# Another order for the first 48 steps of a fused attention and two-FFN kernel, with one weight stage split in two

## The chip, the cores and the metric

The kernel runs on one core of a Trainium2 chip. The metric is the device time of one execution in microseconds (us), the median of three runs. TensorE is called PE, VectorE DVE, ScalarE ACT, GpSimd POOL and SyncE SP, as in the profile.

## The reference

```python
scores = scale * q_c @ k_c.T                 # chunks of 64 tokens, 8 batches x 8 heads x 576 tokens
attn = softmax(scores);  x = attn @ v_c      # then laid out as 4608 tokens x 512
h = x @ w_in                                 # 512 -> 2048
P = a[0] + a[1]*h + a[2]*h**2 + a[3]*h**3
Q = 1.0 + abs(b[0])*abs(h) + abs(b[1])*h**2
x = (P / (Q + 1e-6)) @ w_out                 # 2048 -> 512
h = x @ w_in2;  g = s * relu(h)**2 + b2
out = g @ w_out2                             # 4608 x 512, float32
```

Weights, activations and outputs are float32. Each factor of a large product is split in a high and a low part, and a product is three matmuls: high x high, high x low, low x high.

## The kernel before

Tokens lie in 9 blocks of 512, each of four attention tiles of 128 tokens. A **step** is one block with one of 16 slices of 128 hidden columns. In the first FFN, step n has `mm1` (12 matmuls of 128x512 into one of three PSUM banks, L530 to L532), an element-wise chain that makes the rational function out of that bank, and `mm2` (12 matmuls into four accumulator banks, L548). The first 48 steps are blocks 0 and 1 with slices 0 to 7, block 2 with all 16, and the second halves of blocks 1 and 0.

No scheduler sets the order there. The table `START` is a list of tokens that `play` runs from the left; each token makes the instructions of one stage, each engine's queue gets its own in the order of the list, and semaphores hold an instruction until its inputs are there and its buffer is free. The tokens that matter, with their number:

- loads (512 KB each, v loads 256 KB in four issues): `P` q and k rows of an attention tile, `Q` the same in 16 small issues (L269), `L` and `o` its v rows (L282), `w` a weight slice. They are issued by SP, or by ACT with an `A` behind. A weight slice lies in one of four staging buffers, `wst`, until its sum is done.
- weight slice: `f` takes its absolute value on ACT (`w_abs`, L445) and scales its low words (`w_low`, L449); `g` on DVE for a pair of slices: clamp (L456), shift (L460), and top bits for each (L463); `c` the sum on POOL (L466); `d` the high part on ACT (L473); `D` or `G` the low part on DVE or POOL (L477).
- attention tile: `T`, `q`, `k` transposes and their copies (`X`, two transposes on DVE at L327, for later tiles); `S` scores; `s` maxima (L349) and subtraction (L356) by halves; `e` exponential; `m` sums; `n` normalisation on POOL, with `D` on DVE (L377); `A`, `a` transposed weights (PE, L383); `V` product with v; `v` its copy on ACT; `u` its low part on DVE (L424).
- step n: `M` mm1; `B`, `t` the absolute value and the numerator's start on ACT; `r` the denominator in two instructions on POOL (L634, L637), or with `p` and `rh` the first on ACT, or with `D` both on DVE; `l`, `E` logarithm and exponential on ACT, which divide; `b`, `N` five DVE instructions on the numerator and the quotient, of which `Nc` (L683, output `t`) is the last that reads the step's PSUM bank; `H` the high part gh on ACT; `y` the low part gl on POOL or, with `D`, on DVE (L697); `R` mm2.

With three banks, mm1 of step n+3 waits for `Nc` of step n. mm1 of steps 0 to 7 needs the four tiles 0 to 3, and so `u0` to `u3`.

The stage that the change splits reads:

```python
def w_ends(st, w):
    w_abs(st, w)
    w_low(st)
```

After step 47 come a loop body (`LOOP`) for the steps to 127, a second table (`TURN`) and a planner for the second FFN.

Of the kernel before, what the change touches and what calls it, by code (L numbers as in the profile page):

```python
# [33 lines left out]
    "w0 w1A f0 P4 w2 f1 P1 g1Pa g1Pb g1Pc c0 d0 T4a L1A T1x q1 k1 g1Pd D0 f2 S1y s1b c1 d1 w3 q4 s1d s1a k4 w4 w5 "  # L34
    "f3 P3 S4b s1c e1 s4b g3Pa g3Pb s4d T3d G1 g3Pc g3Pd m1a c2 m1b m1c P2 f4 c3 n1D f5 w6A d2 g5Pa P5 q3 s4a g5Pb "
    "P0 d3 s4c w7 g5Pc x0 e4 m4a g5Pd A1a k3 T2b c4 c5 a1 V1a S3x q2 s3b k2 d5 s3a d4 G3 s3c S2b s3d e3 w8 v1 D4 "
    "s2b L4 u1 T5d s2a G2 k5 G5 q5 L3A T0x q0 w9 s2c k0 S5a m4b S0x m4c s2d s5a n4 s5b f6 m3a P6 m3b A4d a4 s5c w10 "
    "s0a m3c s0b s5d f7 V4d s0d L0 g7Pa n3 f8 g7Pb g7Pd s0c e2 e5 A3b m5a P7A e0 f9 a3 g7Pc v4 T6b m0a q6 m5b g9Pa "
    "m5c V3c k6 c6 g9Pb n5D m2a w11 g9Pc m0b u4 m0c w12 n0D w13 Q8 c8 A5b S6a s6b L5 L2A c7 L6 T7b w14 d6 a5 w15 "
    "m2b d7 v3 m2c k7 q7 g9Pd s6a c9 s6d s6c e6 D7 m6a A0d u3 a0 d8 w16 Q9 d9 n2 S7b m6b G6 A2a a2 V2a s7a m6c f10 "  # L40
    "v2 u2 V0c v0 L7 G8 f11 u0 M0 w17 f12 g11Pa o8 M1 o9 g11Pb w18 f13 g11Pc G9 g11Pd t0 n6 c11 w19 g13Pa B0 c10 p0 "
    "r0h Q10 A6c d11 M2 s7b w20 b0a g13Pb t1 B1 p1 W0 b0b X8 b1a l0 V5a r1h E0 g13Pc s7c c12 s7d b1b e7 t2 S8b M3 "
    "N0a d10 l1 d12 s8a G11 a6 G12 m7a v5 B2 N0b f14 m7b E1 D10 N0c m7c b2a u5 n7 A7x b2b g13Pd r2 H0 s8b V6a M4 "
    "N1a s8d y0 f15 N1b v6 s8c l2 N1c t3 u6 H1 c13 g15Pa E2 b3a Q11 R0 B3 d13 N2a e8 a7 y1 g15Pb N2b D13 M5 N2c r3 "
    "B4 X9 p4 r4h t4 b3b R1 l3 M6 g15Pc g15Pd c14 H2 l4 y2 E3 f16 b4a N3a f17 b4b E4 N3b V7y c15 B5 p5 r5h m8a d14 "
    "G14 N3c g17Pa H3 t5 d15 B6 l5 y3 v7 R2 N4a N4b m8b t6 N4c g17Pb o10 b5a m8c b5b E5 n8 u7 g17Pd A8c c17 p6 r6h "
    "N5a a8 H4 N5b w21A M7 f18 l6 Q12 B7 f19 d17 S9y o11 D15 N5c g17Pc y4D c16 H5 s9a b6a s9c g19Pa b6b G17 s9b E6 "
    "R3 d16 p7 r7h g19Pb t7 y5D M8 g19Pc R4 t8 N6a b7a N6b s9d B8 X10 G16 l7 b8a N6c f20 f21 r8 o12 R5 g19Pd M9 c19 "
    "e9 b7b H6 E7 b8b g21Pa N7a t9 y6 B9 c18 m9a l8 N7b p9 r9h E8 N7c w22A H7 d19 g21Pb R6 m9b g21Pc M10 b9a d18 "
    "N8a l9 b9b c20 N8b m9c B10 y7D g21Pd E9 t10 N8c p10 N9a R7 M11 b10a c21 j7 i7 H8 N9b B11 b10b S10b N9c V8a n9 "  # L50
    "O7 r10h y8 w23A d21 s10a s10b X11 l10 s10c A9y v8 M12 s10d a9 e10 u8 V9b G18 S11a E10 t11 m10a N10a H9 G19 r11 "
    "w24 m10b v9 w25 w26 m10c B12 N10b n10 N10c s11a o13 l11 s11b s11d s11c Q13 u9 b11a f22 e11 d20 m11a f23 t12 "
    "m11b b11b E11 A10y H10 g23Pa M13 b12a r12 g23Pb m11c a10 t13 N11a N11b B13 R8 y9 l12 R9 N11c g23Pd V10y y10 "
    "n11 R10 g23Pc v10 M14 H11 A11x c23 b12b b13a p13 r13h E12 u10 b13b l13 N12a M15 E13 N12b t14 N12c y11 B14 D20 "
    "R11 H12 c22 d22 N13a a11 N13b N13c y12 V11y R12 b14a d23 t15 b14b w27A r14 H13 b15a l14 B15 D23 E14 N14a G22 "
    "v11 G21 u11 N14b M16 M17 r15 N14c b15b f24 f25 g25Pa l15 g25Pb y13D E15 g25Pd B16 r16 N15a f26 g25Pc R13 t16 "
    "f27 N15b M18 N15c g27Pa B17 H14 y14 b16a b16b H15 p17 r17h l16 t17 b17a E16 b17b N16a N16b l17 y15D c25 c24 "
    "t18 E17 R14 d24 B18 N16c g27Pb r18 g27Pd b18a N17a R15 d25 j15 N17b c27 N17c i15 g27Pc b18b H16 l18 H17 M19 "
    "c26 B19 E18 M20 w28A X12 N18a y17D y16 N18b D24 N18c t19 b19a w29A H18 B20 t20 r19 R16 l19 b19b R17 b20a r20 "
    "b20b E19 M21 y18 D25 N19a N19b l20 f28 E20 N20a N19c t21 B21 H19 R18 d27 f29 r21 b21a l21 d26 M22 b21b N20b "  # L60
    "N20c M23 O15 g29Pa E21 H20 B22 y19D w30A t22 D26 y20D N21a t23 R19 N21b N21c r22D b22a D27 b22b w31 B23 l22 "
    "b23a g29Pb E22 H21 Q14 r23 M24 N22a f30 y21 N22b N22c B24 l23 R20 b23b t24 r24 R21 E23 b24a M25 N23a N23b b24b "
    "H22 l24 E24 M26 N23c N24a y22 f31 g31Pa B25 g29Pd t25 R22 H23 b25a N24b r25 N24c H24 B26 l25 b25b g29Pc y23 "
    "E25 M27 y24 p26 r26h N25a R23 N25b t26 b26a t27 B27 b26b M28 N25c g31Pb l26 b27a E26 N26a r27 R24 H25 c28 M29 "
    "l27 y25D b27b N26b N26c E27 M30 t28 d28 b28a B28 b28b N27a R25 N27b N27c g31Pd H26 r28 B29 c29 l28 y26D t29 "
    "p29 r29h E28 D28 H27 B30 b29a c31 d29 l29 N28a b29b N28b N28c r30 g31Pc y27 G29 H28 E29 N29a c30 R26 M31 R27 "
    "t30 l30 B31 p31 r31h y28D N29b b30a d30 t31 M32 Y0 b30b E30 N29c N30a l31 d31 N30b N30c b31a b31b H29 t32 E31 "
    "N31a y29 B32 G30 H30 y30 Q15 b32a R28 b32b M33 p32 r32h B33 l32 N31b t33 R29 N31c E32 r33D l33 N32a H31 N32b "
    "M34 R30 b33a N32c y31 t34 B34 H32 M35 b33b b34a E33 b34b N33a t35 S12y N33b N33c r34D G31 l34 X13 s12b s12a "
# [12 lines left out]
)
# [1530 lines left out]
```

## Time and profile before

| | |
|---|---|
| median of 3 runs | 1639.31 us (1637.15 to 1641.09) |
| profiled execution | 1639.77 us, span 1638.0 us |
| PE busy | 1586.5 us, 97% |
| DVE busy | 1338.1 us, 82% |
| ACT busy | 1128.0 us, 69% |
| POOL busy | 608.8 us, 37% |
| moved by DMA | 263.93 MB, mean 161 GB/s |

The span runs from the first to the last instruction of the profiled execution. An engine's busy time is a sum over the whole program; where it could be faster must be read stretch by stretch. A row of the timeline gives in brackets how long the engine had been idle before the instruction, and what released it. The mean of a group of instructions is from start to end of one; two in a row can overlap by some hundredths of a microsecond.

### The profile page before, as it was taken

Reading aid. Unit: us, or ns where it says so; the run is one execution under the profiler, and the core shown is the slowest. Engines: PE = TensorE matmul, PEld = TensorE weight load, DVE = VectorE, ACT = ScalarE, POOL = GpSimd, SP = SyncE. Lnnn points to the kernel's source line nnn. Section 1 sums busy time; section 2 is a strip of 40 time slices with the busy share of each in tenths; the row PEclk is TensorE's granted clock in tenths of the full one; section 3 lists DMA queues with packets and bytes.
Section 4 is the critical chain, followed back from the end, with each engine's and each line's share of the span. In section 5 each row is a group of like instructions: output and inputs, shape, how many; then the busy total and the mean of one; then the engine's idle time right before and its main releaser. Section 6 shows DMA issues by size and latency. Waiting matters only on the chain.

```text
span 1638.0 us, 26407 instructions
## 1 busy us (share of the span) xinstructions
PE 1586.5 (97%) x9068; PEld 1293.9 (79%) x9068; DVE 1338.1 (82%) x2165; ACT 1128.0 (69%) x1909; POOL 608.8 (37%) x513
## 2 busy tenths in 40 slices
PE   4699999999999999999999999999999999999998
PEld 3577887777878888888888788888888888888886
DVE  6899988899888988888779987668867886788676
ACT  5788766667677686867678776657665756676554
POOL 3677565347577676757557510000000000000000
PEclk9799999999999999999999999999999999999999
DMA  9655302344263553625034587865589649666853
GB/s 232 158 158 147 93 1 65 84 113 134 66 167 87 154 141 83 196 65 133 3 123 135 206 272 238 324 231 174 164 208 303 233 130 297 213 220 161 279 169 86
DMA packets 365526, 263.93 MB, mean 161 GB/s; under 512 B 276816, under 2 KB 315728, under 8 KB 364880
## 3 DMA queue, kind: packets, MB, share of 16 engines
q1 hardware_dynamic: 352720, 255.55, 53.0%
q10 hardware_dynamic: 12672, 6.69, 1.5%
q8 instruction: 72, 1.18, 0.3%
q14 instruction: 62, 0.51, 0.1%
HBM read 201.33 MB, written 60.82 MB: 160 GB/s over the span
## 4 chain that ended last, share of the span: by engine, by line
PE 79%; DVE 6%; DMA 4%; ACT 4%; issue 3%; POOL 2%; SPq 2%; ACTq 0%; DVEq 0%; POOLq 0%
PE acc L548 20%; PE ae L1107 16%; PE hA L1046 11%; PE h L530 7%; PE h L532 6%; PE h L531 6%; PE hE L1046 5%; PE hc L1046 3%; PE hc L1107 3%; DMA wst<-in_moe_w_in_dram 1%; SPq L269 1%; DMA vs<-in_v_dram 1%; PE pat L383 1%; DVE ah L679 1%; PE pat L408 1%
## 5 line engine op out<-in xcount | busy, mean ns | idle before, releaser
L1107 PE MATMUL ae<-gs,wo 128*128 128x512 f32 x1152 | 294.0, 391 | 1.7 <-DVE acc L1126 0.7
L548 PE MATMUL acc<-gh,w 128*128 128x512 f32 x1152 | 288.0, 392 | 0.0
L530 PE MATMUL h<-xh,w 128*128 128x512 f32 x640 | 256.1, 400 | 8.9 <-DVE t L683 8.0
L1107 PEld LDWEIGHTS ae<-gs,wo 128*128 128x128 f32 x1152 | 215.8, 188 | 49.5 <-DVE acc L1126 1.1
L531 PE MATMUL h<-xl,w 128*128 128x512 f32 x640 | 251.0, 392 | 0.0
L532 PE MATMUL h<-xh,w 128*128 128x512 f32 x640 | 251.0, 392 | 0.0
L548 PEld LDWEIGHTS acc<-gh,w 128*128 128x128 f32 x1152 | 214.1, 188 | 44.4 <-ACT gh L691 0.2
L637 POOL TENSOR_TENSOR r<-r,ah 128x512 f32<-128x512 f32 x130 | 174.3, 1341 | 77.6 <-ACT r L632 65.0
L1046 PE MATMUL hA<-xs,wi 128*128 128x512 f32 x768 | 195.6, 390 | 0.7 <-ACT g L1057 0.7
L697 POOL TENSOR_TENSOR gl<-t,gh 128x512 fp32r<-128x512 f32 x111 | 147.7, 1333 | 100.0 <-ACT gh L691 58.4
L1046 PEld LDWEIGHTS hA<-xs,wi 128*128 128x128 f32 x768 | 144.1, 188 | 31.8 <-ACT g L1057 1.1
L1085 DVE TENSOR_TENSOR gs<-g,gs 128x512 fp32r<-128x512 f32 x224 | 146.4, 684 | 15.1 <-ACT gs L1081 14.5
L548 PE MATMUL acc<-gl,w 128*128 128x512 f32 x576 | 154.8, 390 | 2.0 <-POOL gl L697 1.9
L1081 ACT ACTIVATE gs<-g 128x512 fp32r<-128x512 f32 x224 | 132.7, 624 | 28.2 <-DVE g L1077 27.8
L530 PEld LDWEIGHTS h<-xh,w 128*128 128x128 f32 x640 | 121.2, 189 | 39.1 <-DVE t L683 12.4
L532 PEld LDWEIGHTS h<-xh,w 128*128 128x128 f32 x640 | 121.0, 189 | 26.0
L531 PEld LDWEIGHTS h<-xl,w 128*128 128x128 f32 x640 | 121.2, 189 | 24.2 <-DVE xl L424 0.3
L623 ACT ACTIVATE t<-h,a_sb 128x512 f32<-128x512 f32 x144 | 111.1, 773 | 38.1 <-PE h L532 18.1
L548 PEld LDWEIGHTS acc<-gl,w 128*128 128x128 f32 x576 | 107.6, 188 | 26.5 <-POOL gl L697 4.2
L679 DVE SCALAR_TENSOR_TENSOR ah<-r,h 128x512 f32<-128x512 f32 x144 | 98.1, 681 | 37.1 <-ACT h L668 35.7
L1128 DVE TENSOR_TENSOR acc<-ae,acc 128x512 f32<-128x512 f32 x112 | 77.0, 689 | 61.3 <-PE ae L1107 60.3
L663 ACT ACTIVATE ah<-r,lnb 128x512 f32<-128x512 f32 x144 | 103.6, 719 | 32.8 <-POOL r L637 26.5
(143 smaller groups left out, 2964.9 us busy)
## 6 DMA issues: line engine op xcount, KB each, us to landing
wi<-wq SPq DMA_DIRECT2D x112, 512.0 KB, 4.3
wo<-wq SPq DMA_DIRECT2D x112, 512.0 KB, 4.8
wst<-in_moe_w_in_dram SPq DMA_DIRECT2D x28, 512.0 KB, 5.3
wst<-in_moe_w_out_dram SPq DMA_DIRECT2D x27, 512.0 KB, 4.7
wi<-wp SPq DMA_DIRECT2D x16, 512.0 KB, 4.0
wq<-wc SPq DMA_DIRECT2D x32, 256.0 KB, 2.8
w<-wi SPq DMA_DIRECT2D x16, 512.0 KB, 6.6
raw<-x2d SPq DMA_DIRECT2D x16, 512.0 KB, 7.4
```

The costliest lines, as they stand in the source:

```text
L530: T.matmul(h, wh, xh[:, kk], start=kk == 0, stop=False)
L531: T.matmul(h, wh, xl[:, kk], start=False, stop=False)
L532: T.matmul(h, wl, xh[:, kk], start=False, stop=kk == KD - 1)
L548: T.matmul(o, l, r, start=first and n == 0, stop=last and n == 2)
L623: A.activation(t1, h_t[i], AF.Identity, scale=a_sb[:, 3:4], bias=a_sb[:, 2:3])
L637: eng.tensor_tensor(out=r, in0=r, in1=ah, op=ALU.mult)
L679: V.scalar_tensor_tensor(out=t, in0=r, scalar=ONE, in1=y, op0=ALU.add, op1=ALU.mult)
L697: (eng or (G if i < N1 else V)).tensor_tensor(out=gl, in0=tmp.pop(i)["g"], in1=f(g_t[i][0]), op=ALU.subtract)
L1046: T.matmul(ps[b], w[:, l, z * P:(z + 1) * P], x[:, z], start=n == 0 and p in (1, 2, 5), stop=n == 5, skip_group_check=True)
L1081: A.activation(gx[t, s, k][0][:, 0], gt[t, s, c], AF.Copy)
L1085: V.tensor_tensor(out=g[:, 1], in0=gt[t, s, c], in1=f(g[:, 0]), op=ALU.subtract)
L1107: T.matmul(o, w[:, e, l, dp * P:(dp + 1) * P], gx[t, 2 * u + e, k][0][:, g], start=n == 0 and p in (1, 2, 5), stop=n == 5, skip_group_chec ...
```

## The change

The table `START` is replaced by another list, said to be found for varied durations with full transfer queues counted. It makes the same stages for the same tiles, slices and steps, with two kinds of difference besides the order. Some stages change engine: `n` on DVE goes from 6 to 1, `y` on DVE from 15 to 8, `r` on DVE from 4 to 1, first instruction of `r` on ACT from 19 to 16, `D` from 13 to 11, all to POOL; weight loads that ACT issues go from 9 to 14. And `w_low` of the first FFN's slices is no longer in `f`: it is a token of its own, `h` with a letter behind.

```diff
 START = (
-    "w0 w1A f0 P4 w2 f1 P1 g1Pa g1Pb g1Pc c0 d0 T4a L1A T1x q1 k1 g1Pd D0 f2 S1y s1b c1 d1 w3 q4 s1d s1a k4 w4 w5 "
+    "w0A w1 w2 f0 f1 h1b h0b g1Pa g1Pb g1Pc g1Pd c0 c1 P2 d0 d1 P4 T2c q2 P1 G0 T4a f2 k2 w3 q4 S2d s2b P3 w4A x0 "
...
-    def w_ends(st, w):
-        w_abs(st, w)
-        w_low(st)
...
-            w_ends(st, w)
+            w_abs(st, w)
+            if phase:
+                w_low(st)
             words[n] = phase, kind, i, st, w
...
-        do["h"] = lambda n, _: w_get(n)
+        do["h"] = lambda n, x: w_low(words[n][3]) if x else w_get(n)
```

What the lists make of it stands here at three places, first before, then now. Lines of the changed kernel are up to three lower or one higher. SP's queue where it issues the v rows of tile 0 (`wst` is a weight slice, `qk` the q or k rows of a tile, `vq` v rows); before, where row 29 is those v rows:

```order
27 L253 DMA qk<-in_k_dram 128x8x64
28 L436 DMA wst<-in_moe_w_in_dram 128x4x256
29 L282 DMA vq<-in_v_dram 64x4x64 x4
30 L441 DMA wst<-in_moe_w_out_dram 128x1024
31 L436 DMA wst<-in_moe_w_in_dram 128x4x256
32 L441 DMA wst<-in_moe_w_out_dram 128x1024
33 L269 DMA qk<-in_q_dram 32x8x32 x8
34 L269 DMA qk<-in_k_dram 32x8x32 x8
35 L282 DMA vq<-in_v_dram 64x4x64 x8
```

and the part of SP's queue in the changed kernel that ends with them, in row 30:

```order
22 L442 DMA wst<-in_moe_w_out_dram 128x1024
23 L270 DMA qk<-in_q_dram 32x8x32 x8
24 L270 DMA qk<-in_k_dram 32x8x32 x8
25 L283 DMA vq<-in_v_dram 64x4x64 x4
26 L254 DMA qk<-in_q_dram 128x8x64
27 L254 DMA qk<-in_k_dram 128x8x64
28 L283 DMA vq<-in_v_dram 64x4x64 x4
29 L437 DMA wst<-in_moe_w_in_dram 128x4x256
30 L283 DMA vq<-in_v_dram 64x4x64 x4
```

Before, the 16 small issues of tile 8 stand behind the v rows of tile 0; now they stand ahead of them, with two other sets of v rows, a tile's q and k rows and a weight slice between.

DVE around `u0` (the last `xl<-pat,xh`), where the rows after it lead to step 0's `b` (`t<-t,h`); before:

```order
78 L424 TENSOR_TENSOR xl<-pat,xh 128x4x64 x2
79 L424 TENSOR_TENSOR xl<-h,xh 128x4x64
80 L424 TENSOR_TENSOR xl<-pat,xh 128x4x64
81 L456 TENSOR_SCALAR w<-w 128x1024
82 L460 TENSOR_SCALAR w<-w 128x1024
83 L463 SCALAR_TENSOR_TENSOR w<-wst,w 128x512 x2
84 L456 TENSOR_SCALAR w<-w 128x1024
85 L349 TENSOR_REDUCE mx<-pat 128x4
86 L657 TENSOR_TENSOR t_878<-t_878,h 128x512
```

and now:

```order
62 L425 TENSOR_TENSOR xl<-h,xh 128x4x64
63 L425 TENSOR_TENSOR xl<-pat,xh 128x4x64
64 L474 TENSOR_TENSOR w_3_749<-w,w_3_749 128x512
65 L453 TENSOR_SCALAR w<-w 128x1024
66 L457 TENSOR_SCALAR w<-w 128x1024
67 L350 TENSOR_REDUCE mx<-pat 128x4
68 L460 SCALAR_TENSOR_TENSOR w<-wst,w 128x512 x2
69 L453 TENSOR_SCALAR w<-w 128x1024
70 L654 TENSOR_TENSOR t_873<-t_873,h 128x512
```

`u0` stands some 17 rows nearer to the start of DVE's queue, and about as many weight and attention instructions as before lie between it and step 0.

POOL where step 0's denominator is made (`e<-e,sm` is a normalisation, `w<-w,wst` a weight sum, `r` a denominator); before:

```order
20 L477 TENSOR_TENSOR w_3_743<-w,w_3_743 128x512
21 L377 TENSOR_TENSOR e<-e,sm 128x512
22 L466 TENSOR_TENSOR w<-w,wst 128x512 x2
23 L637 TENSOR_TENSOR r<-r,ah 128x512 x2
24 L466 TENSOR_TENSOR w<-w,wst 128x512
25 L477 TENSOR_TENSOR w_4_914<-w,w_4_914 128x512
26 L477 TENSOR_TENSOR w_7_1010<-w,w_7_1010 128x512
```

and now:

```order
27 L378 TENSOR_TENSOR e<-e,sm 128x512
28 L631 TENSOR_SCALAR r<-ah,ab_sb 128x512
29 L634 TENSOR_TENSOR r<-r,ah 128x512
30 L463 TENSOR_TENSOR w<-w,wst 128x512 x2
31 L474 TENSOR_TENSOR w_6_909<-w,w_6_909 128x512
32 L474 TENSOR_TENSOR w_4_984<-w,w_4_984 128x512
33 L463 TENSOR_TENSOR w<-w,wst 128x512 x2
34 L634 TENSOR_TENSOR r<-r,ah 128x512 x2
```

Step 0's denominator is now wholly on POOL, and six weight instructions stand between it and those of steps 1 and 2, where before steps 0 and 1 stood together.

## Rows read from the trace of the kernel before

**Rows 1.** The page: PE's busy time, and its busy tenths in 40 slices.
```profile
PE 1586.5 (97%) x9068; PEld 1293.9 (79%) x9068; DVE 1338.1 (82%) x2165; ACT 1128.0 (69%) x1909; POOL 608.8 (37%) x513
...
PE   4699999999999999999999999999999999999998
```

**Rows 2.** Stretches: us, busy PE, PEld, DVE, ACT, POOL, clock, DMA share, GB/s.
```profile
0.00:60.84 60.84, 31.47 (x505) 24.16 (x505) 42.42 (x87) 37.81 (x73) 27.75 (x27) 0.86 0.87 216
60.84:139.25 78.41, 70.59 (x561) 56.50 (x561) 74.80 (x133) 67.09 (x119) 59.36 (x47) 0.93 0.55 140
139.25:179.65 40.40, 40.40 (x240) 32.98 (x239) 36.28 (x61) 33.36 (x59) 27.21 (x23) 1.00 0.38 109
179.65:353.01 173.36, 172.01 (x1013) 138.40 (x1012) 146.82 (x237) 116.85 (x192) 93.81 (x77) 1.00 0.29 75
```

**Rows 3.** Timeline of PE: start, us, instruction, in brackets the idle time before.
```profile
60.84 0.79 PE L530 MATMUL h<-xh,w 128*128 128x512 f32 x1 [0.80 <-ACT xh L416]
...
77.43 0.79 PE L530 MATMUL h<-xh,w 128*128 128x512 f32 x1 [3.41 <-DVE t L683]
...
96.79 0.50 PE L530 MATMUL h<-xh,w 128*128 128x512 f32 x1 [0.49 <-DVE t L683]
...
138.84 0.66 PE L383 MATMUL pat<-ident,e 128*128 128x128 f32 x4 [1.40 <-POOL e L377]
...
293.54 0.27 PE L339 MATMUL h<-qkT 64*64 64x64 f32 x2 [0.49 <-DVE t L683]
...
359.54 0.50 PE L530 MATMUL h<-xh,w 128*128 128x512 f32 x1 [0.93 <-DVE t L683]
```

**Rows 4.** Waits of DVE up to 61 us: total, times, longest.
```profile
DVE w L456 <- ACT w L445: 6.9, 1, 6.9
DVE mx L349 <- PE pat L339: 4.5, 2, 3.6
```

**Rows 5.** Groups by line to 350 us: busy us, mean ns, idle before.
```profile
L637 POOL TENSOR_TENSOR r<-r,ah 128x512 f32<-128x512 f32 x44 | 59.7, 1356 | 27.3 <-ACT r L632 23.1 <-DVE t L657 2.1
...
L466 POOL TENSOR_TENSOR w<-w,wst 128x512 int32<-128x512 int32 x32 | 44.6, 1400 | 33.8 <-DVE w L463 17.9 <-ACT w L445 3.8 <-DVE sm L371 3.5
L697 POOL TENSOR_TENSOR gl<-t,gh 128x512 fp32r<-128x512 f32 x32 | 43.3, 1354 | 37.7 <-ACT gh L691 18.9 <-PE acc L548 11.7 <-DVE e L356 5.2
...
L463 DVE SCALAR_TENSOR_TENSOR w<-wst,w 128x512 int32<-128x512 int32 x32 | 25.7, 815 | 0.1
...
L634 POOL TENSOR_SCALAR r<-ah,ab_sb 128x512 f32<-128x512 f32 x25 | 21.4, 855 | 30.5 <-ACT ah L617 30.3
...
L477 DVE TENSOR_TENSOR w<-w,w 128x512 fp32r<-128x512 f32 x13 | 12.7, 976 | 2.0 <-ACT w L473 2.0
L377 POOL TENSOR_TENSOR e<-e,sm 128x512 f32<-128x512 f32 x11 | 12.0, 1087 | 5.4 <-DVE sm L373 4.7 <-ACT gh L691 0.7
...
L327 DVE STREAM_TRANSPOSE qkT<-qk 128x512 f32<-128x512 f32 x18 | 11.7, 684 | 0.0
L456 DVE TENSOR_SCALAR w<-w 128x1024 f32<-128x1024 f32 x16 | 11.2, 697 | 7.0 <-ACT w L445 6.9
L697 DVE TENSOR_TENSOR gl<-t,gh 128x512 fp32r<-128x512 f32 x14 | 11.0, 787 | 0.0
...
L349 DVE TENSOR_REDUCE mx<-pat 128x4 f32<-128x256 f32 x25 | 10.0, 413 | 5.7 <-PE pat L339 4.7 <-PE h L339 1.0
...
L377 DVE TENSOR_TENSOR e<-e,sm 128x512 f32<-128x512 f32 x5 | 5.3, 1051 | 0.1
```

**Rows 6.** SP: its longest wait up to 61 us, and issues of `Q8`.
```profile
SPq L436 <- POOL w L466: 8.6, 2, 7.4
...
55.61 3.55 SPq L269 DMA_DIRECT2D qk<-in_q_dram  x7
...
61.15 3.90 SPq L269 DMA_DIRECT2D qk<-in_k_dram  x8
```

**Rows 7.** Timeline: POOL and DVE at the subtraction of L477.
```profile
31.79 4.19 POOL L477 TENSOR_TENSOR w<-w,w 128x512 fp32r<-128x512 f32 x3
...
33.12 1.73 DVE L477 TENSOR_TENSOR w<-w,w 128x512 fp32r<-128x512 f32 x1 [0.16 <-ACT w L473]
```

95 rows, old and new, of the table START are left out of this document.

## Prediction

> **What bounds the kernel now.** I read the slices of the page first [rows 1]: TensorE (PE) is at 9 tenths or more from the third slice to the last but one, so over 37 of 40 slices only its own work counts, and it can be shortened only where it waits. Its busy time is 1586.5 of 1638.0 us. The 51.5 us left are almost all in the part that the change rewrites. The table by stretch [rows 2] says where: up to 60.84 us, where the first matmul of step 0 starts (I call the start of the first matmul of step n "Mn"), PE is busy 31.47 us; from M0 to M13 it is busy 70.59 of 78.41; from M13 to M19 it is never idle; from M19 to M48 it lacks 1.35 of 173.36.
>
> Who holds it up is in the timeline [rows 3]: M3 and M6 each start after a wait for `DVE t L683`, the last vector instruction of a step three earlier, which gives that step's PSUM bank back. So look next at DVE in the same table [rows 2]: 74.80 of 78.41 busy from M0 to M13. In that stretch DVE is the bound and PE follows it. From M13 on DVE has air (36.28 of 40.40, then 146.82 of 173.36) and PE is the bound. Before M0 neither is: DVE is busy 42.42 of 60.84, its longest waits being 6.9 us for the first weight and 4.5 for PE [rows 4], and behind those stand the transfers, at 87% of their engines and 216 GB/s [rows 2]. So three questions make the sum: when M0 starts, how much DVE work lies between M0 and M13, and which small waits are left after that. After step 48 the order is untouched.
>
> The profiled execution took 1639.77 us, a span of 1638.0 and 1.77 around it; the median is 1639.31, 0.46 lower. I make the sum against 1639.77 and take 0.46 off at the end. About 0.2%, 3.3 us, can be told from no change.
>
> **1. The start of step 0.** M0 needs all four attention tiles of token block 0; the last vector instruction for it is `u0` (L424), and DVE works in order, so M0 comes after all DVE work listed before `u0`. Counted over the two lists up to `u0`, the change takes away three normalisations (n on DVE, L377, 1.05 us each, [rows 5]: 3.15) and five of the half-tile softmax instructions (0.41 each: 2.07), adds one tile's two transposes at L327 (2 x 0.68: 1.37), and has one softmax sum less, three small instructions that I put at 0.6: together 4.5 us less. With the same 18.4 us idle, M0 would be at 60.84 - 4.5 = 56.3. The other gate is the last transfer that M0 needs. In the new list this is `L0`, the v rows of tile 0; ahead of it and with it stand w0 to w10, P0 to P7 and Q8 (20 loads of 512 KB) and five v loads of 256 KB, 11,520 KB or 11.8 MB; at 216 GB/s they are through at 54.6, and the second product of tile 0, the copy on ACT and `u0` follow in some 2.3 us: 56.9. I take **56.6, 4.2 earlier**. Bounds: the last v loads stand on SP behind sixteen issues of Q8, which took 0.5 us of SP each [rows 6], behind L4, and behind w10, which waits for its buffer; SP's longest waits so far are for exactly that (8.6 us on `POOL w L466`, [rows 6]). If these give the whole gain back, M0 stays at 60.8. On the other side, DVE has 11.5 us of idle time besides the first 6.9; a third less and M0 is at 52.5.
>
> The split of the weight's first stage (`w_low` now placed by itself as `h`) is in this term. The 32 instructions of L449 stay on ACT, but the clamp on DVE no longer stands behind two of them. What hides them now is that the POOL sum (L466) needs them only after three DVE instructions. If ACT is late with one, POOL waits, and the buffer and the next load with it. ACT also issues 14 weight loads in place of 9; ACT does nothing else while one waits for its buffer. I cost both at nothing beyond the bounds above.
>
> **2. From M0 to M13.** M13 needs the bank of step 10. Between `u0` and `N10c`, the last DVE instruction of step 10, the two lists have the same 33 instructions of steps (three for each of 0 to 10), the same b, u and D. The change has five softmax halves more here (2.07), one weight pair more (clamp 0.70, shift about the same, and twice 0.82: some 3.05), one normalisation more (1.05), one tile's transposes less (1.37) and one gl less on DVE (0.79), [rows 5]: **4.0 us more**. It is work that was not done before M0. Against it stand 3.6 us in which DVE is idle in this stretch now [rows 2], most of it waiting just after M0 for steps 0 to 2; the new list puts more than ten weight and softmax instructions between `u0` and `N0c`, which can fill these waits, so I let 2.1 of it go and keep 1.5. Both ends, all of it kept and none, are in the range. The stretch then takes 78.4 + 4.0 - 2.1 = 80.3, and M13 is at 136.9 in place of 139.25: of the 4.2 us only **2.35** are left.
>
> **3. From M13 to M19** PE is the bound in both [rows 2]: six mm1 and eight mm2 in both lists, and one transposition of the attention weights more (0.6 to 0.66, [rows 3]): 2.35 - 0.6 = 1.75 left.
>
> **4. After M19.** Over the whole list DVE gives up seven gl (0.79 each) and five normalisations (1.05), and some smaller things: 10.8 us by these two alone. From step 16 to 46 each step's last DVE instruction then stands behind less DVE work than now, where from M19 to M48 26.5 of 173.4 us are idle already. So the four short waits for DVE, the longest of them 0.49 us [rows 3], 1.2 together, should go, and so should the 0.93 at M50: **2.1 us**. What is late next is POOL, which takes these over: five normalisations at 1.09, seven gl at 1.35, and six more first halves (0.86) and three more second halves (1.36) of the denominator, [rows 5], 24 us on an engine that is busy 93.8 of 173.4 us there [rows 2]. It has room on average, and I cost this at nothing.
>
> Sum: 1.75 + 2.1 = 3.9 us less; 1639.77 - 3.9 - 0.46 = **1635.4**.
>
> **Rivals.**
> *POOL becomes the bound between M0 and M13 (slower).* POOL is busy 59.36 of 78.41 us there now. The new list adds there two weight sums and two low parts of weights (L466, L477, some 1.4 us each), a gl (1.35) and two whole denominators (2.21) in place of three second halves (1.36), and takes a normalisation out (1.09): 6.2 us more, 84%. A step's chain runs ACT, POOL, ACT, DVE, so a late POOL makes every third bank late. And DVE itself lengthens beside a busy POOL: at 33.12 us DVE took 1.73 us for the subtraction at L477, POOL being in L477 from 31.79 on; the mean on DVE is 976 ns, against 787 for the same form at L697 [rows 5, 7]. If all 6.2 us come to lie on the path, M13 is at 143.1, the rest of POOL's load keeps the 2.1 us of waits alive, and with 0.65 for the transposition the kernel ends 4.5 later, at 1643.8. With the 2.1 us kept alive the result is 1.8 us less plus what is exposed: the gain is gone from 1.8 us exposed, and the kernel is slower by over 0.2% from 5.1. The Trainium skill, "SBUF — State Buffer", section "Who interferes with whom", has a rule for this: a DVE instruction with two SBUF inputs and a GpSimd one that reads SBUF exclude each other for a whole instruction. The row at 33.12 us agrees with it (1.73 us). By that rule the moved subtractions no longer exclude POOL from DVE's side, while those that stay meet a POOL that is busier; no run here shows what of the 6.2 us would meet one, so it changes neither the price nor the chance. Chance of this rival 0.14.
>
> *All of the early start is eaten (no change).* DVE is saturated from M0 to M13, and the work not done before M0 is 4.0 us; if the 3.6 us idle stay, M13 is at 56.6 + 78.4 + 4.0 = 139.0, as now. Then 0.25 - 0.65 + 2.1 = 1.7 us are won: 1637.6. Chance 0.28.
>
> *The idle time shrinks too (much faster).* M0 at 52.5 and no DVE idle to M13: 4.1 + 1.5 more, 1629.8. For it speaks that eleven of the 18.4 idle us are waits between engines in a list where three pairs of stages stand close together. Against it: transfers at 87%. Chance 0.18.
>
> That the list leaves out or repeats work is ruled out by counting: step for step the two hold the same operations, apart from the engine of some and the split stage.
>
> **Chances and range.** Forecast, 3 to 6 us faster or a little less, 0.40. Faster by over 0.2%: 0.18, and 0.34 of the forecast's (its own spread goes below 3.3 at times): 0.52. Slower: 0.12 of the POOL rival's 0.14, and 0.02 for a late SP load: 0.14. Within 0.2%: 0.34. Range 1629.0 (the faster rival, and a little of the loop's waits) to 1642.0 (most of the way to the POOL rival).
>
> **What would show it.** In the trace after: M0 near 56.6, with `L0`'s landing just before; DVE busy about 38 us up to it; M3 near 72 and M6 near 95, still waiting for DVE; M13 near 137; no DVE wait of PE from M19 to M50. Wrong, if M0 is at 60 or later (SP), if M3 to M13 wait for an instruction whose releaser is POOL, or if gl on POOL holds mm2 (L548) up.

## The result: slower, and the profile after

The changed kernel takes 1649.92 us (median of 4, 1648.35 to 1652.21), the kernel before 1640.2 beside it: a ratio of 1.0064, 95% interval 1.005 to 1.0078. The profiled execution took 1648.81 us with a span of 1647.0, 9.0 us more than before.

I cut both traces at M0, M19, M48 and M51. At M19, M48 and M51 the two orders have done the same matmuls; at M0 nearly so (the old list has one tile's four transpositions more, and the scores of another tile). Single steps between don't compare. Nor does M22, which I first took for a common point: the old list has the 12 matmuls of step 18's `mm2` ahead of it, the new one behind. The expectations below still speak of M22; I use it only among versions of one list. After M51 the difference hardly changes. The table by stretch, first the two stretches of the kernel before that [rows 2] does not have, then the changed kernel (columns: stretch, its length, then for PE, PEld, DVE, ACT and POOL busy us and count; the granted clock, where 1.00 is the 2.4 GHz level; DMA share; GB/s):

```profile
60.84:179.65 118.81, 110.99 (x797) 89.48 (x798) 111.08 (x192) 100.45 (x177) 86.58 (x69) 0.95 0.49 130
353.01:369.66 16.65, 15.72 (x130) 12.55 (x128) 16.12 (x26) 9.93 (x17) 6.58 (x6) 1.00 0.50 114
```

```profile
0.00:63.11 63.11, 32.60 (x501) 25.89 (x501) 35.35 (x80) 36.38 (x70) 29.62 (x28) 0.82 0.93 213
63.11:188.64 125.53, 112.40 (x802) 89.17 (x801) 116.07 (x198) 101.03 (x178) 99.17 (x77) 0.97 0.51 129
188.64:359.13 170.49, 170.29 (x1013) 138.55 (x1011) 136.43 (x216) 115.17 (x189) 102.86 (x89) 1.00 0.26 68
359.13:379.22 20.09, 17.11 (x135) 13.58 (x129) 17.70 (x28) 11.68 (x18) 7.75 (x7) 0.92 0.49 103
```

Read the lengths first: +2.3 to M0, +6.7 from M0 to M19, -2.9 from there to M48, +3.4 from M48 to M51, together 9.6 (0.6 of it comes back later). From M19 to M48 the new list gains: for the same 1013 matmuls PE idles 0.20 us in place of 1.35. DVE has 10.4 us less to do there and POOL 9 more, and PE is the bound. Then read DVE (third engine) up to M19: it is busy 151.4 us in place of 153.5, so the list does take work off it; but it idles 37.2 (188.64 less 151.42) in place of 26.2 (179.65 less 153.50). That is the loss.

How well does a stretch repeat? Three profiles of the changed order (this one and two of experiment 6, whose edits come after 330 us) have M0 at 62.56 to 63.52 and M19 at 188.64 to 190.85; three of the old order have them at 60.13 to 60.95 and 178.82 to 179.65. So up to M19 differences of 1 or 2 us say little. From M19 to M48 an order repeats to 0.1 us.

The waits of DVE up to M0 (answering to [rows 4]; columns: total us, times, longest), one of the kernel before, then the changed one:

```profile
DVE xl L424 <- ACT xh L416: 1.6, 1, 1.6
```

```profile
DVE xl L425 <- ACT xh L417: 7.7, 4, 3.2
DVE w L453 <- ACT w L446: 6.8, 1, 6.8
DVE mx L350 <- PE h L340: 5.8, 1, 5.8
DVE sm L369 <- ACT e L363: 3.9, 2, 3.5
```

The second is the first weight, as before. The first has grown by 6.1 us: `u` waits for `v`, which waits for the product with the v rows, and those come late. The issues of `L0` before; then SP's queue in the changed kernel and the last wait of PE ahead of M0 (columns: start, us, what; x8 is eight issues in a row):

```profile
46.89 2.58 SPq L282 DMA_DIRECT2D vq<-in_v_dram  x4
```

```profile
33.11 7.96 SPq L270 DMA_DIRECT2D qk<-in_q_dram  x8
41.12 5.30 SPq L270 DMA_DIRECT2D qk<-in_k_dram  x8
46.46 2.58 SPq L283 DMA_DIRECT2D vq<-in_v_dram  x4
50.36 3.05 SPq L283 DMA_DIRECT2D vq<-in_v_dram  x4
54.10 2.58 SPq L283 DMA_DIRECT2D vq<-in_v_dram  x4
60.10 0.33 PE L409 MATMUL pat<-eT,vq 64*64 64x64 f32 x2 [1.15 <-DMA vq<-in_v_dram]
```

Q8's sixteen issues hold SP from 33.1 to 46.4, 13.3 us, and the three sets of v rows that M0 needs (L1, L4, L0) go out behind them; the last, `L0`, at 54.1 to 56.7, 7.2 us later than before. I had written them through at 54.6.

### The profile page after: what moved, and what is told of

The parts are those of the page before. It is cut to its first block, busy times and chain, and to the rows that moved or that the text cites. A ratio compares the mean times of both kernels' runs of the same rounds, so it can differ in the third digit from the quotient of the medians.

```text
span 1647.0 us, 26450 instructions
## 1 busy us (share of the span) xinstructions
PE 1587.4 (96%) x9068; PEld 1296.6 (79%) x9068; DVE 1326.9 (81%) x2145; ACT 1126.5 (68%) x1906; POOL 633.4 (38%) x536
## 4 chain that ended last, share of the span: by engine, by line
PE 78%; DVE 5%; DMA 5%; POOL 3%; ACT 3%; SPq 3%; issue 3%; DVEq 0%; POOLq 0%; ACTq 0%
PE acc L545 19%; PE ae L1104 16%; PE hA L1043 11%; PE h L527 7%; PE h L529 6%; PE h L528 6%; PE hE L1043 5%; PE hc L1043 3%; PE hc L1104 2%; DMA wst<-in_moe_w_in_dram 2%; DMA qk<-in_q_dram 1%; SPq L270 1%; POOL r L634 1%; PE pat L409 1%; SPq L283 1%
## 5 line engine op out<-in xcount | busy, mean ns | idle before, releaser
L694 POOL TENSOR_TENSOR gl<-t,gh 128x512 fp32r<-128x512 f32 x118 | 157.0, 1333 | 82.7 <-ACT gh L688 55.0
L1125 DVE TENSOR_TENSOR acc<-ae,acc 128x512 f32<-128x512 f32 x112 | 77.1, 690 | 60.8 <-PE ae L1104 59.8
L620 ACT ACTIVATE t<-h,a_sb 128x512 f32<-128x512 f32 x144 | 111.2, 772 | 18.9 <-PE h L529 12.1
```

Of the source, the lines that this page charges most:

```text
L620: A.activation(t1, h_t[i], AF.Identity, scale=a_sb[:, 3:4], bias=a_sb[:, 2:3])
L694: (eng or (G if i < N1 else V)).tensor_tensor(out=gl, in0=tmp.pop(i)["g"], in1=f(g_t[i][0]), op=ALU.subtract)
```

## The experiments

Each edit moves tokens of `START` or changes their engine letters; a line of the diffs is the piece of the list. Times are medians; before, measured beside them, lies between 1638.9 and 1639.9.

**1. Where Q8 stands.** First the token alone.

```diff
-... m4b c4 Q8 d4 m3c ... w10 g7Pb L0 w11 ...
+... m4b c4 d4 m3c ... w10 g7Pb L0 Q8 w11 ...
```

> The changed kernel with one token moved: Q8 (16 small loads) stands behind L0, the v rows of tile 0, and no longer five loads ahead of them. Theory (the queue ahead of L0): in the changed kernel SP issues Q8 from 33.1 to 46.4 us and the pieces of L0 only from 54.1 to 56.7; without these 13.3 us the pieces go out some 10 us earlier, M0 comes at 56 to 58 in place of 63.1, and since VectorE's work up to step 10 stays what it is, M13 moves by the same 5 to 6 us: 1644 to 1645 us. Rival (POOL is the bound from M0 to M13): M0 comes earlier, but M13 stays near 146 and the time at 1648 to 1650. Second rival (the transfers themselves are the limit, not their order in the queue): M0 stays at 61 to 63 and the time at 1648 to 1650.

1655.52 us, ratio 1.0093 (1.0076 to 1.011): slower still, M0 at 66.68. All three expectations missed. DVE's timeline shows why:

```profile
57.95 0.71 DVE L328 STREAM_TRANSPOSE qkT<-qk 128x512 f32<-128x512 f32 x1 [9.33 <-DMA qk<-in_k_dram]
61.47 0.71 DVE L328 STREAM_TRANSPOSE qkT<-qk 128x512 f32<-128x512 f32 x1 [2.81 <-DMA qk<-in_k_dram]
```

These are X8, the transposes of those rows. The new list has X8 ahead of `u0`, so a later Q8 holds DVE itself. Q8 must be moved with its consumers.

```diff
-... Q8 d4 ... X8 V1b ... f13 S8b s6b ... b0b M1 ... S7a b1a ...
+... d4 ... L0 Q8 w11 ... b0b X8 M1 ... S7a S8b b1a ...
```

> The changed kernel with all of tile 8's early part behind the first token block: Q8 stands behind L0, its two VectorE transposes X8 behind b0b (after M0, about where the old list has them), its scores S8 behind S7a. The run with Q8 alone moved had VectorE wait 9.3 and 2.8 us for these loads at X8, ahead of u0, which hid what the queue does. Theory (SP's queue ahead of L0 holds M0): M0 at 57 to 59 in place of 63.1, M13 at 140 to 142 in place of 146.2, the time 1644 to 1646 us. Rival (the transfers as a whole limit the start, whatever their order): M0 at 61 to 63, 1648 to 1650.

1651.59 us, ratio 1.0074 (1.0056 to 1.0092). M0 comes at 56.74, just ahead of the theory's 57 to 59, but M3 at 84.46 and M22 at 206.54. SP's issues of Q8 (51.3 to 61.5) now stand ahead of `w11`, and DVE waits for that weight slice by way of ACT:

```profile
DVE w L453 <- ACT w L446: 8.7, 1, 8.7
```

So the next run puts Q8 two slices further back:

```diff
-... L0 Q8 w11 D5 g7Pc h7b c6 w12 w13 g7Pd ...
+... L0 w11 D5 g7Pc h7b c6 w12 w13 Q8 g7Pd ...
```

> As the run with Q8, X8 and S8 moved, but with Q8 two weight slices further back, behind w13, where the old list has it. In that run M0 came at 56.74, and then SP's 10 us of issues for Q8 held w11: ACT waited 8.6 us for that slice and VectorE 8.7 for ACT, and M13 came at 150.5. Theory (whatever stands behind Q8 on SP pays its 10 us): M0 at 56 to 58, no such wait for a weight slice, M13 at 139 to 142, 1643 to 1645 us. Rival (VectorE would have waited after M0 anyway, for step 0's and 1's chains): M13 at 145 to 150, 1648 to 1651.

1645.81 us, ratio 1.0034 (1.0022 to 1.0046), 4.1 below the changed kernel. M0 is at 56.24, the long wait for a weight is gone, and M22 is at 198.51 in place of 202.24. It ends 0.8 us above the top of the theory's range, and M13, at 142.44, 0.4 above its; the hand-over to the loop took 22.0 us in it, 1.9 more than in the changed kernel (more on that below). The mirror, the old list with Q8 alone moved forward:

```diff
-... G3 s3c S2b s3d e3 w8 v1 D4 s2b L4 ... w13 Q8 c8 ...
+... G3 s3c S2b s3d e3 w8 v1 D4 s2b Q8 L4 ... w13 c8 ...
```

> The old kernel with one token moved the way the change moves it: Q8 from behind w13 to directly ahead of L4. L4, T0's rows behind w9, w10 and L0 then stand behind 16 more issues of SP. X8 stays where it is, after M0. Theory (SP's issues of Q8 are what the v rows of tile 0 wait for): L0 goes out 5 to 10 us later, M0 at 64 to 70 in place of 60.8, and the time 1643 to 1649 us. Rival (the order on SP matters little, the rest of the new list makes its M0 late): M0 within 1 us of 60.8, 1639 to 1641.

1646.26 us, ratio 1.004 (1.0025 to 1.0055): one token makes the old kernel 6.7 us slower. M0 is at 67.83, PE waits up to it 9.8 us in three waits for v rows (the longest 8.3), and every later stretch is as in the old kernel to 0.15 us:

```profile
0.00:67.83 67.83, 32.65 (x504) 25.59 (x504) 41.88 (x86) 37.67 (x73) 28.09 (x27) 0.85 0.87 205
67.83:186.52 118.69, 110.57 (x797) 88.98 (x797) 111.36 (x193) 100.67 (x177) 85.99 (x69) 0.96 0.45 123
```

Here a late M0 is not won back. The bytes that go ahead of the v rows don't make 7.0 us: an estimate from Q8's 0.52 MB and the 205 GB/s of the first row is 2.6.

**2. The weight loads that ACT issues.**

```diff
-w0A w1 ... w4A ... w5A ... w8A ... w9A ... w24A ... w25A ... w27
+w0 w1A ... w4 ... w5 ... w8 ... w9 ... w24 ... w25 ... w27A
```

> The changed kernel with the old issuers for the weight loads: nine by ACT in place of fourteen, the rest by SP. Theory (SP's queue limits the opening): w8 and others come back to SP, ahead of Q8 and the v rows, M0 1 to 3 us later, 1650 to 1653 us. Rival (ACT's waits for a buffer ahead of a load cost more than SP's queue): M0 and M13 1 to 3 us earlier, 1647 to 1649.

1673.39 us, ratio 1.0203 (1.0185 to 1.022). The direction of the theory, but 23.5 us in place of 1 to 3: I had thought only of the opening. There M0 is 5 us later; at M14 PE waits 14.4 us. SP's queue, then ACT, DVE and PE:

```profile
148.73 10.10 SPq L283 DMA_DIRECT2D vs<-in_v_dram  x8
158.93 4.00 SPq L270 DMA_DIRECT2D qk<-in_q_dram  x8
162.97 4.63 SPq L270 DMA_DIRECT2D qk<-in_k_dram  x8
167.70 1.88 SPq L605 DMA_DIRECT2D x2d<-o  x4
169.67 0.70 SPq L437 DMA_DIRECT2D wst<-in_moe_w_in_dram  x1
172.89 1.15 ACT L470 ACTIVATE w<-w 128x512 fp32r<-128x512 f32 x2 [15.97 <-DMA x2d<-o]
178.20 0.69 DVE L453 TENSOR_SCALAR w<-w 128x1024 f32<-128x1024 f32 x1 [16.08 <-ACT w L446]
181.06 0.80 PE L527 MATMUL h<-xh,w 128*128 128x512 f32 x1 [14.44 <-DVE t L680]
```

v rows that wait for their buffer, tile rows and a block's stores go first, the slice at 169.67 and the next wait behind them, and DVE behind the two slices. ACT stands still too, for 16.0 us, behind its own load of `w27`, which the edit gave it and which by the profile waits for those stores. So the run takes seven loads off ACT and puts two on it, and does not tell what each costs; with the issuers of the new list this order is 23.5 us faster than with the old.

**3. The engines of `n` and `y`**, first the old ones in the new order, then the new ones in the old order (five normalisations and seven `gl` net).

```diff
-n1 n0 n5 n7D n13 n15 n16 y2D y4 y5 y11D ... y46
+n1D n0D n5D n7 n13D n15D n16D y2 y4D y5D y11 ... y46D
```

> The changed kernel's order with the old engines for n and y: five normalisations and seven gl go back from POOL to VectorE over the list. Theory (POOL has room, VectorE's idle time ahead of M0 is the loss): M13 within 1 us of 146.2; M50's wait for VectorE shorter, as y46 and n16 are among them, by 0.5 to 1; 1648 to 1650 us. Rival (POOL's added work is the loss): M13 at 141 to 143 and the time 1644 to 1646.

1656.17 us, ratio 1.01 (1.0084 to 1.0116): 6.3 slower than the changed kernel. My rival that POOL's added work makes the loss is refuted; the theory's "no difference" is wrong too. From M0 to M22 DVE is busy 134.3 us in place of 127.05, and the stretch takes 145.4 in place of 139.1.

> The old order with the new engines for n and y: five normalisations and seven gl go from VectorE to POOL, three of the normalisations before M13. In the new order, taking this back made it 6 us slower. Theory (the new engines are worth something, the new order costs more): VectorE has 3 us less up to M13 and M13 comes 1 to 3 us earlier: 1636 to 1639 us. Rival (POOL is late at three normalisations, as at 138.8 us in the old kernel, where TensorE waits 1.40 for it): 1640 to 1643.

1647.23 us, ratio 1.005 (1.0033 to 1.0066): 7.6 slower than before. The rival's direction, and more. Each order wants its own engines. In this pair only letters differ, so the groups of DVE by line up to 200 us show what POOL's work does to DVE, the old kernel first (columns: count, then busy us and mean ns of one):

```profile
L456 DVE TENSOR_SCALAR w<-w 128x1024 f32<-128x1024 f32 x15 | 10.5, 698 | 7.0 <-ACT w L445 6.9
L460 DVE TENSOR_SCALAR w<-w 128x1024 int32<-128x1024 int32 x14 | 10.4, 742 | 0.2
L371 DVE TENSOR_SCALAR sm<-sm 128x8 f32<-128x8 f32 x12 | 4.7, 388 | 0.1
```

```profile
L453 DVE TENSOR_SCALAR w<-w 128x1024 f32<-128x1024 f32 x14 | 11.5, 824 | 6.9 <-ACT w L446 6.8
L457 DVE TENSOR_SCALAR w<-w 128x1024 int32<-128x1024 int32 x14 | 11.6, 831 | 0.2
L372 DVE TENSOR_SCALAR sm<-sm 128x8 f32<-128x8 f32 x12 | 5.5, 459 | 0.1
```

The same instructions take 126, 89 and 71 ns longer in the mean; from M0 to M22 (the same matmuls in these two) DVE is busy 131.05 us in place of 126.40 although, net, three `gl` have left that stretch; one normalisation, `n7`, has come to it (1.49). Up to M0, which three normalisations have left (3.15 us), DVE is busy 41.70 in place of 42.42. So work taken off DVE came back in part as longer DVE instructions. The other part of the loss is at single steps that wait for a later `gl` or normalisation: from M22 to M48 it takes 159.6 us, 2.9 more.

**4. The split of `w_low`**, undone in the new order.

```diff
-... f6 S5d m4c ... h6b L4 ...
+... f6 h6b S5d m4c ... L4 ...
```

> The changed kernel with the second of its changes undone: each h of a weight slice stands directly behind its f, so that the absolute value and the scaling of the low words are one stage again. I costed the split at nothing. Theory (it is worth nothing, ACT is not the limit): M0 within 1 us of 63.1, 1649 to 1651 us. Rival (the split keeps ACT and POOL in step with the weight buffers): M0 1 to 3 us later and 1651 to 1654 us.

1653.69 us, ratio 1.0087 (1.0071 to 1.0103): 3.8 slower than the changed kernel, as the rival has it, though not where it has it, and the two intervals overlap (that one's is 1.005 to 1.0078). M0 is at 63.36, 0.25 later; DVE idles 17.5 us from M0 to M22 in place of 12.1 (12.5 and 14.9 in the two repeats of the changed order). The split seems to be worth something here. I take it that on ACT the steps' instructions can now stand between the two halves of a weight's first stage; no run isolates that.

**5. Halves of one list behind halves of the other.**

```diff
-(the new list)
+(new_head_old_rest: new up to u0, then what is left in the old order)
+(old_to_M3_new_rest, old_to_M19_new_rest: old up to M3 or M19, then what is left in the new order)
```

> The new list up to u0, and behind it the old list without the tokens already done, engines included. Theory (the loss is made before M0: VectorE idles 27.8 us up to M0 in place of 18.4, and that time can't be had back): M0 near 63, M13 at 146 to 149, the end of the list as before the change: 1647 to 1650 us. Rival (POOL's added work from M0 to M13 makes the loss): that work is gone here, M13 at 140 to 142, and the time 1641 to 1643.

1652.54 us, ratio 1.0076 (1.0061 to 1.0091), 2.5 us over the theory's range. M0 is at 66.54, 3.4 later than with the new list to the end, and M19 at 193.02, with old engines on POOL (99.8 us busy from M0 to M22), so POOL's added work isn't needed for a loss.

> The other way round: the old list up to M3, and behind it the new list without what is done, with the new engines. Theory (idle time before M0): M3 at 77.4 as before the change, M13 at 137 to 140, M19 to M48 2.9 us shorter than before, the hand-over to the loop 3.4 longer: 1637 to 1641 us. Rival (POOL's added work from M0 to M13): POOL's work is that of the new list, M13 at 143 to 146, 1645 to 1648.

1657.42 us, ratio 1.0106 (1.0089 to 1.0122); M3 is at 76.71, M13 at 152.69, outside both. The theory falls here: an old opening does not save the new rest.

> The old list up to M19, and behind it the new list without what is done, with its engines. Theory (the new list loses before M19, wins after it and loses again at the hand-over to the loop): M19 at 179.7 as before the change, M19 to M48 in 170.5 us in place of 173.4, M48 to M51 in 20.1 in place of 16.7: 1640 to 1641 us. Rival (the 2.9 us after M19 are only catching up of what was late at M19): M19 to M48 in 173 us, 1643 to 1644.

1648.42 us, ratio 1.0057 (1.0042 to 1.0073): outside both. At the seam PE waits 4.75 us at M21, and M19 to M48 takes 179.3 us. Behind the seam the new list is as quick as in the changed kernel. From M23 to M48, with the same matmuls in all three, the kernel before, the changed one and this run:

```profile
199.22:353.01 153.79, 152.64 (x929) 122.82 (x929) 128.72 (x210) 102.45 (x169) 79.40 (x65) 1.00 0.26 68
207.68:359.13 151.45, 151.25 (x929) 122.78 (x927) 121.54 (x196) 102.06 (x168) 87.79 (x75) 1.00 0.25 63
206.55:358.13 151.58, 151.40 (x929) 122.84 (x928) 121.86 (x196) 102.30 (x168) 87.75 (x75) 1.00 0.24 63
```

So the gain behind M19 is the new list's own and no catching up; the seam costs more. A list fits its own start, and these three runs say little on which half is at fault; the next groups do.

**6. The hand-over to the loop.** `M50`, the loop's third step, waits for DVE before the change [rows 3] (0.93) and after:

```profile
367.85 0.80 PE L527 MATMUL h<-xh,w 128*128 128x512 f32 x1 [2.98 <-DVE t L680]
```

Two suspects: X16 and Q17 late, or the scores of tile 16, which the new list has behind R45. The first run moves both.

```diff
-... t46 N44c b45a ... N46a N45c X16 Q17 a15 ... u15 R45 S16x s16a ...
+... t46 N44c X16 Q17 b45a ... N46a N45c a15 ... u15 S16x R45 s16a ...
```

> The changed kernel with two places of the end of the list put nearer to the old order: X16 and Q17 stand directly behind N44c (before: six VectorE instructions of steps later, behind N45c), and S16 stands ahead of R45 on TensorE in place of behind it. Theory (the hand-over to the loop is late because the scores of tile 16 and the q and k rows of tile 17 come late, which hold the logarithm of step 47 on ACT and step 47's last instructions on DVE): M50's wait for DVE falls from 2.98 to under 1.0 us, and M48 to M51 from 20.1 to 16.7 or 17: 1646 to 1647 us. Rival (it is the normalisation, gl and denominator on POOL at the end of the list, y46, r47, n16): M50 waits 2 to 3 us as now, 1649 to 1650.

1649.7 us, ratio 1.0066 (1.0044 to 1.0088). M48 to M51 takes 17.06 us, about as expected, and M50 waits 1.35 where I had under 1.0, but M22 to M48 takes 1.5 more: S16 ahead of R45 waits 1.41 us for `u15` (`xl`). So the scores stay, and SP's queue is looked at (the changed kernel):

```profile
337.92 10.84 SPq L283 DMA_DIRECT2D vs<-in_v_dram  x8
348.80 0.60 SPq L554 DMA_DIRECT2D o<-x2d  x1
350.93 2.65 SPq L605 DMA_DIRECT2D x2d<-o  x4
353.67 5.46 SPq L270 DMA_DIRECT2D qk<-in_q_dram  x8
359.18 4.17 SPq L270 DMA_DIRECT2D qk<-in_k_dram  x8
```

The row at 337.92 is `o15` and, from 346.2, `o16`: SP stands still for 5.7 us between them, as `o16` waits for its buffer. The loads of J47, the stores of O39 and Q17 wait behind it, and in the loop's first rows DVE waits 1.48 us for Q17's rows. Before the change Q17 went out at 345.0.

```diff
-... N35b o16 H34 ... t46 N44c b45a ... N45c X16 Q17 a15 ...
+... N35b H34 ... t46 N44c X16 Q17 o16 b45a ... N45c a15 ...
```

> The changed kernel with X16, Q17 and o16 standing in this order directly behind N44c; S16 stays behind R45. In the changed kernel SP waits from 340.5 to 346.2 us for a buffer for the v rows o16, and the loads of J47, the stores of O39 and the 16 issues of Q17 stand behind it; Q17 goes out at 353.7 (before the change at 345.0, 8 us ahead of M48). Theory (the hand-over is late because SP is held by o16, and VectorE then by Q17's rows): Q17 goes out near 347, VectorE's transposes of tile 17 don't wait, M50's wait falls from 2.98 to 0.5 or 1.5, M48 to M51 from 20.1 to 17 or 17.5, with M45 to M48 unchanged at 27.5: 1646.5 to 1647.5 us. Rival (it was the scores of tile 16 behind R45, which the first run on this place moved as well): M48 to M51 stays at 19 to 20 us, 1649 to 1650.

1647.4 us, ratio 1.0041 (1.0028 to 1.0055). Q17 goes out at 347.78, M50 waits 1.37, M48 to M51 takes 17.21 and M22 to M48 156.91, as the theory has it. The run moves X16 as well, which no run moves alone. In the run before, X16 stood as here, Q17 went out at 354.70, and PE's two waits together were 2.76 us, near the 2.98; that speaks for the queue, but does not isolate it.

**7. Both repairs together.**

> The changed kernel with the two repairs that each helped alone: Q8 behind w13 (with X8 and S8 behind M0), which brought 4.1 us, and X16, Q17 and o16 behind N44c, which brought 2.5. Theory (they lie in stretches that don't touch each other and add up): M22 near 198.5, M48 to M51 17.2 in place of 22.0 there: 1641 to 1643 us, still behind the kernel before. Rival (they don't add, as the hand-over's wait gives TensorE's backlog time): 1644 to 1646.

1642.1 us (10 runs), ratio 1.0021 (1.0012 to 1.0031): within the theory's range, 3.2 us slower than the kernel before. Of the changed kernel's time the two repairs take 7.8 us. Its stretches:

```profile
0.00:55.30 55.30, 29.66 (x468) 23.07 (x468) 33.16 (x76) 35.46 (x69) 29.24 (x28) 0.81 0.99 226
55.30:184.15 128.85, 113.30 (x833) 89.70 (x833) 116.63 (x202) 101.94 (x179) 99.58 (x78) 0.96 0.52 133
184.15:354.62 170.47, 170.28 (x1014) 138.55 (x1012) 136.45 (x216) 115.22 (x189) 103.08 (x89) 1.00 0.27 71
354.62:371.83 17.21, 15.84 (x134) 12.65 (x128) 16.35 (x27) 10.98 (x18) 7.61 (x7) 1.00 0.37 75
```

M0 is 5.5 us ahead of the old kernel, M19 is 4.5 behind it, M48 1.6. Two more places of Q8, with the repaired end, ask whether X8 is why M0's lead goes; first Q8 behind `L5`, with X8 behind `b0b`, then X8 behind M3 and S8 and its maxima behind that (the diff shows the second).

```diff
-... w13 Q8 g7Pd ... L6 L5 m1b ... b0b X8 M1 ... S7a S8b ... M3 l2 ...
+... w13 g7Pd ... L6 L5 Q8 m1b ... b0b M1 ... S7a ... M3 X8 l2 ...
```

> Both repairs together: Q8 behind L5 (two sets of v rows further back than behind w13), X8 and S8 behind M0 as there, and the end of the list as in the run with o16 late. Theory: M0 at 56 to 57; the v rows of tiles 5 and 6 no longer stand behind Q8's issues, so that M3's 2.4 us for them shrink to about 1 and M22 is at 196 to 198; M22 to M48 156.9 as in every run; M48 to M51 at 17: 1639 to 1641 us, level with the kernel before. Rival (the time M0 gains is lost again up to M22, since VectorE has the same work): M22 at 198.5 to 200, and 1641 to 1644.

1645.59 us, ratio 1.0037 (1.0024 to 1.0049). M0 is at 55.52, but X8 waits 2.87 and 3.79 us for its rows, M3 is at 80.92 and M22 at 204.57: outside both expectations.

> As the run with Q8 behind L5, but X8 stands behind M3 and S8 and its maxima behind it. There X8 on VectorE waited for rows that landed at 63 to 68 us, TensorE waited 6.2 us for VectorE at 70.9, and M3 came at 80.92 although M0 was at 55.52. Theory (what is left between M0 and M22 in these runs is again Q8, now by its consumer): no such wait, M3 at 73 to 76, M22 at 195 to 198, 1638 to 1641 us. Rival (VectorE's work between M0 and M22, 128 us in this list against 126.4 in the old, sets the stretch whatever stands first): M22 at 198.5 or later, 1641 or more.

1642.31 us (10 runs), ratio 1.0017 (1.0008 to 1.0027). X8 no longer waits and M3 is at 73.71, as the theory has it; but M22 is at 197.96, the last of the theory's range and near the rival's, and the time is the rival's. With no wait for Q8's rows at X8 any more, the early M0 is still gone by M19, which is at 184.36 (179.65 before).

**8. A version that beats both?** A place late in the old list where the change's idea, less work for DVE, meets a wait for DVE is M50 [rows 3].

```diff
-... m16c b47a b47b n16D y46D
+... m16c b47a b47b n16 y46
```

> The old kernel with two engine letters of the change at the very end of the list: n16 and y46 go from VectorE to POOL, all else as it was. With all n and y of the change the old order had no wait at M50 and M48 to M51 took 15.29 us in place of 16.65. Theory (the change's idea is right for the hand-over, where VectorE's last instructions hold step 47): M50's wait of 0.93 goes, M48 to M51 15.3 us, 1638 to 1638.5 us, 0.1% faster, at the limit of what can be told. Rival (POOL is late with n16 or gl 46): 1640 or more.

1638.56 us (11 runs) beside 1639.69, ratio 0.9991 (0.9982 to 1.0). M50 has no wait and M48 to M51 takes 15.28 us, as expected:

```profile
352.16:367.44 15.28, 15.28 (x129) 12.42 (x128) 14.76 (x25) 10.51 (x17) 9.48 (x8) 1.00 0.50 99
```

Some 1.1 us, at the edge of what can be told: the lowest median of these kernels, 11 us below the changed one, but hardly to be told from the kernel before.

## Why the prediction was wrong, point by point

*Start of step 0: 56.6 forecast, 63.11 measured.* Two steps failed. "With the same 18.4 us idle" took DVE's idle time as a property of the kernel. DVE's work up to M0 did shrink, by 7.1 us, more than the 4.5 I counted; its idle time rose by 9.3. And the other gate, "through at 54.6", let all transfers flow at the mean rate and left out that an issue takes SP's time and can wait: the rate nearly held (213 GB/s up to M0), but `L0` was not issued before 54.1 to 56.7, and PE waited for it until 60.10. I had named this place as the bound ("sixteen issues of Q8, which took 0.5 us of SP each"), some 8 us on a queue with room; in the changed kernel the sixteen held SP for 13.3 us, and M0 fell behind even the upper bound of 60.8, which the prediction had as a sign of being wrong ("at 60 or later"). With Q8 behind w13 M0 is at 55.3 to 56.2. That is near the forecast, partly by luck, as the forecast counted Q8's bytes ahead of `L0`.

*M0 to M13.* DVE has 4.15 us more to do (78.95 in place of 74.80), as counted (4.0). What failed is that 2.1 us of idle would be filled: DVE idles 4.2 us there, in place of 3.6.

*M13 to M19* took 2.0 us more in place of 0.6. "PE is the bound in both" failed: PE idles 1.06 us there, 0.99 of it in one wait for DVE at 151 us.

*After M19.* The short waits on DVE went, as forecast, and this step was right: M19 to M48 is 2.9 us shorter, 1.15 of it waits (1.2 forecast) and the rest PE busy time for the same 1013 matmuls, which I had not forecast and no run explains. M50 went from 0.93 to 2.98 in place of zero. I looked only at DVE's load there, not at what SP's queue holds: the failed step is "so should the 0.93 at M50".

*The rivals.* "POOL becomes the bound" had the right sign and half the size (4.5 against 9.7) for a wrong reason: with the old engines the new order is slower. Half of its text was right, though. DVE instructions do lengthen beside POOL (experiment 3), and that keeps the moved work from paying. "All of the early start is eaten" is what the repaired list does, and more: M0 5.5 early, M19 4.5 late.

*The split* was costed at nothing; undoing it costs 3.8 us by the medians in this order. ACT's loads were costed at nothing; giving them their old issuers costs 23.5.

*Open:* from M0 to M19 the repaired list still takes 128.85 us in place of 118.81. DVE is busy 5.6 us longer there, part of it work that the earlier M0 leaves behind it, and idles 12.2 in place of 7.7. Of these 4.5 us, 4.1 are two waits that the old list does not have there, for rows of a transposition (2.1) and for `v` (2.0). With X8 behind M3 the transposition no longer waits, and M19 is where it was (184.36, 184.15); so what sets it stays open.

## What to carry to other kernels

Where an order moves loads, lay out the issuing engine's queue as you do for a compute engine: each issue with its time, each load that waits for a buffer with all that stands behind it, and each consumer that waits for its rows on another engine. In an in-order queue a load placed early can do as much harm as a late one. And an engine's idle time is not carried over from one order to another: a count of its work says by how much it could be earlier, not that it will be. Compare two orders only between points ahead of which both have done the same work, and count it: here one product of 12 matmuls stands on different sides of M22, and with M22 as a common point the new list's gain behind M19 does not show.

## What the runs showed that I had not expected

*DVE instructions with one input wait for POOL as well.* In the first 200 us of the kernel before, the changed kernel and the old order with new engines, each clamp of a weight pair (128x1024, one input) that starts with POOL idle takes 0.67 to 0.70 us. Of those that start inside a POOL instruction, the ones with under 0.1 us of it left take 0.68 and the others 0.70 to 1.60; there are 2 such others of 15 before, 8 of 14 in the changed kernel. One such pair:

```profile
124.81 1.43 DVE L453 TENSOR_SCALAR w<-w 128x1024 f32<-128x1024 f32 x1
124.40 1.29 POOL L634 TENSOR_TENSOR r<-r,ah 128x512 f32<-128x512 f32 x1
```

POOL ends at 125.69, DVE at 126.24, about as if the clamp had begun when POOL was nearly through. In the prediction I weighed only DVE instructions with two inputs. The Trainium skill, "SBUF — State Buffer", section "Who interferes with whom", has this case too: `tensor_scalar`, if its operands allow, can enter a mode that takes the port pair shared with GpSimd, and then the one of the two that issues second waits for the whole instruction. The rows agree for a DVE that comes second (here the clamp ends 0.55 us behind POOL); no row here shows a POOL that does.

*A queue of issues also waits for its own loads.* Eight small issues of Q8 took 7.96 us at 33 to 41 us in the changed kernel, and 4.05 and 3.90 at 59 to 67 us with Q8 behind L5. Most single issues take 0.45 us in both; what is more at 33 us is two waits of SP for earlier v rows to land:

```profile
SPq L270 <- DMA vq<-in_v_dram: 4.3, 2, 2.5
```

Full transfers alone don't lengthen an issue here: before, seven took 3.55 us [rows 6] with the DMA share at 1.05 in that time. Why an issue waits for these rows no run shows.

*The clock at the hand-over.* From M50 to M51 the same matmuls take 10.12 us before, after PE's wait of 0.93, with the granted clock at 1.00, the 2.4 GHz level. After the wait of 2.98 in the changed kernel they take 11.37 at a mean of 0.87 between the two levels (the other is 1.2 GHz); after 3.65 (Q8 behind w13) 12.63 at 0.77; after 1.37 again 10.10 at 1.00. So the repair that took 1.6 us off that wait made M48 to M51 2.9 us shorter.
